# Half of the moving DFT tiles split by two GpSimd DMAs and a negated ScalarE copy instead of a ScalarE copy and a VectorE subtraction

## The chip, the cores and the metric

The kernel runs on one core of a Trainium2 chip, as one program. The metric is the device time of one execution in microseconds; the runs of the kernel before took 594.92, 598.23 and 600.19 us (median 598.23). A profile of one further execution gives the trace that is read below. The engines of the core are TensorE (PE, matrix products), VectorE (DVE), ScalarE (ACT), GpSimd (POOL) and SyncE (SP), each with its own queue of instructions that it works off in order. DMAs are issued from such a queue, and 16 DMA engines move the data.

## The reference

Two independent halves, whose outputs stand side by side in the last axis.

```python
# A: Fourier mixing, x is [1, 2048, 512]
a = einsum("bsd,ed->bse", x, dft_hid_re)
b = einsum("bsd,ed->bse", x, dft_hid_im)
y = einsum("ts,bse->bte", dft_seq_re, a) - einsum("ts,bse->bte", dft_seq_im, b)

# B: a diagonal state space model as a long convolution, u is [1, 2048, 512], N = 128
dt = exp(log_dt)
A = -exp(log_A_real) + 1j * A_imag
C = (C_real + 1j * C_imag) * dt[:, None]
P = exp((A * dt[:, None])[:, :, None] * pos[None, None, :])
K = 2.0 * einsum("dn,dnl->dl", C, P).real
y = irfft(rfft(u_t, 4096) * rfft(K, 4096), 4096)[:, :, :2048]
y = transpose(y) + u * D_skip
```

All inputs and outputs are float32.

## The kernel before

**The Fourier half (`Fnet`).** It multiplies in the other order than the reference: first `x` with the sequence matrices, then the result with the hidden ones. The sequence matrices come as 128 tiles `sT` of 128x512 (four stretches `t` of 512 output positions, two parts `c`, real and imaginary, 16 tiles `k` along the sequence). For each of the 8 groups `("s", t, c)`, the 16 tiles are the moving operands, the 16 resident `x` tiles the weights, and four PSUM tiles `acc` gather the result, which goes to DRAM as `p`. Four groups `("p", t)` of 8 tiles each follow: there the `p` tiles are moving and the hidden matrices `wT` are the weights. That is 8 x 16 + 4 x 8 = 160 moving tiles. The groups are worked off in the order s (all eight), then p.

Float32 products are made from three matmuls in a rounded 32-bit format, float32r. Every operand is split: `hi` is the operand rounded to float32r, `lo` is the operand minus `hi`, rounded as well. A product is `hi*x_hi + lo*x_hi + hi*x_lo` (L327). One moving tile takes part in 4 x 3 = 12 matmuls of 512 columns, so there are 160 x 12 = 1920 of them.

How a moving tile comes in (`load`, L287 on): SyncE's queue loads it into one of four `raw` buffers; when a slot of the ring of three `hi`/`lo` pairs is free, ScalarE copies `raw` into `hi` (L207) and VectorE writes `lo` as `raw - hi` (L211). The `raw` buffer is free after that, the ring slot after the last of the 12 matmuls.

**The other half (`Ssm`).** VectorE and ScalarE build two tables of powers per chunk of 32 channels (16 chunks; L566, L575, L582 and their neighbours), TensorE multiplies them into taps of the filter (L762), GpSimd adds the skip term to the first tap (L785, eight times), then come a two-stage transform of the taps (L792) and of `u` (L835), products of the spectra (L913 for the second stage, L926 to L942 for the products, L949 for the first inverse stage) and the last inverse stage (L995). Data passes through DRAM between the stages (`xu`, `xk`, `zs`). Its TensorE batches stand between the matmuls of the Fourier half.

**The order of the work.** A planner (`Plan`) runs the kernel as a set of coroutines: each step names an engine and an estimated duration, and the planner takes the step that can begin first, by urgency where several can. The instructions are written in that order, each engine's in the order of its steps. So the order is fixed when the kernel is built, from estimates: a DMA is taken to last 3.3 us (`LATENCY`) beyond its transfer, `load(kb)` is kb/330 us with a least value of 0.55, an ACT copy of 512 columns is 0.525 us. An engine that waits holds up what stands behind it in its own order. Semaphores of the planner stand for buffers: `raws` (4), `ss` (ring slots, `DEPTH`), `acc` (4 PSUM tiles), `ys` (3 staging tiles for evictions).


Of the kernel before, what the change touches and what calls it, by code (L numbers as in the profile page):

```python
# [8 lines left out]
F32 = mybir.dt.float32  # L9
F32R = mybir.dt.float32r  # L10
I32 = mybir.dt.int32
AF = mybir.ActivationFunctionType
OP = mybir.AluOpType
# [3 lines left out]
SEQ, DM, NS = 2048, 512, 128  # L17
# [151 lines left out]
def act(cols):  # L169
    return 0.09 + cols * 0.00085  # L170
# [6 lines left out]
def load(kb):  # L177
    return max(0.55, kb / 330)


class Fnet:
# [83 lines left out]
    def loads(self, b):  # L265
        yield b.uks
        x_raw = b.pool.tile([128, 4, DM], F32, name="uk", bufs=b.n)
        self.x_left = 16
        for g in self.groups:
            for i in self.items[g]:  # L270
                urgency = -1 if i in self.items[self.groups[0]][:3] else 0
                if g == self.groups[0]:
                    if i[3] >= 4:
                        yield self.x_ev[i[3] - 4]
                    if not i[3]:
                        self.plan.spawn(self.load_x0(x_raw[:, 0]), -1)
                    self.plan.spawn(self.load_x1(b, x_raw[:, i[3] % 4], i[3]), urgency)
                if i[0] == "p":
                    k = i[1], i[3] // 4, i[3] % 4
                    yield self.p_ev[k]  # L280
                    src = self.p[k]
                else:
                    src = self.sT[i[1], i[2], i[3]]
                yield self.raws
                self.plan.spawn(self.load(src, None, self.m, i, self.m_ev[i]), urgency)

    def load(self, src, to, where, key, ev):  # L287
        raw = self.pool.tile([128, DM], F32, name="raw", bufs=RAWS)
# [717 lines left out]


CHUNK, FIRST = 32, 128
RAWS, DEPTH, STAGED, AHEAD = 4, 3, 3, 3
BATCH = 2  # L1010


# [70 lines left out]
```

## Time and profile before

| | |
|---|---|
| median of the runs | 598.23 us (594.92 to 600.19) |
| span of the profiled execution | 595.6 us, 16944 instructions |
| TensorE busy | 585.1 us |
| VectorE busy | 495.7 us, 883 instructions |
| ScalarE busy | 381.0 us, 745 instructions |
| GpSimd busy | 5.3 us, 12 instructions |
| mean granted TensorE clock | 0.996 |
| DMA | 125.97 MB, 212 GB/s over the span |

The span is the time from the first to the last instruction of the profiled execution; the page gives no time around it, and the span lies within the times of the runs. "Busy" counts the time in which at least one instruction of an engine was under way; the ends of matmuls are modelled, and their recorded lengths overlap. A group row of the page gives line, engine, operation, destination and sources by name, shapes and count, then total busy time in us and the mean of one in ns, then the idle time of the engine just before these instructions and what ended most of it. A row of waits gives who waited for whom, the total in us, how often, and the longest.

### The profile page before, as it was taken

What the parts mean: (1) busy time and instruction counts of PE and PEld (TensorE: products, weight loads), DVE (VectorE), ACT (ScalarE), POOL (GpSimd) and SP (SyncE); (2) the same over time, 40 slices, a digit from 0 to 9 for tenths busy, and PEclk for the clock granted to TensorE, in tenths of its full rate; (3) what the DMA queues carried; (4) which work ended last, traced back from release to release, by engine and by line L of the source; (5) the groups of instructions that cost most, each with busy time, mean ns of one, the idle gap of its engine ahead of it and who ended that gap; (6) DMA issues with size and microseconds to landing.
All of it is one profiled execution on the core that took longest, in us unless ns stands there. A gap on an engine that the chain in (4) does not pass through costs nothing.

```text
span 595.6 us, 16944 instructions
## 1 busy us (share of the span) xinstructions
PE 585.1 (98%) x6982; PEld 451.6 (76%) x6982; DVE 495.7 (83%) x883; ACT 381.0 (64%) x745; POOL 5.3 (1%) x12
## 2 busy tenths in 40 slices
PE   8999999999999999999899999999989999999997
PEld 6767668788788777777687787778767887777775
DVE  6977989999999999999699999999979973253620
ACT  5789884947586596758374976677655625354522
POOL 0000000000000000000000000000000000000000
PEclk9999999999999999999999999999989999999999
DMA  8999995363593376454778593478668745899674
GB/s 264 321 360 344 333 339 186 107 177 94 128 279 100 102 193 216 141 148 122 237 213 245 149 279 120 132 213 257 207 202 253 249 126 168 223 348 276 204 256 149
DMA packets 141246, 125.97 MB, mean 212 GB/s; under 512 B 46192, under 2 KB 106352, under 8 KB 140912
## 3 DMA queue, kind: packets, MB, share of 16 engines
q1 hardware_dynamic: 140880, 124.48, 68.2%
q8 instruction: 55, 0.90, 0.6%
q10 hardware_dynamic: 288, 0.39, 0.3%
q14 instruction: 23, 0.19, 0.1%
HBM read 82.12 MB, written 42.73 MB: 210 GB/s over the span
## 4 chain that ended last, share of the span: by engine, by line
PE 79%; DVE 12%; DMA 3%; issue 3%; ACT 2%; SPq 0%; DVEq 0%; ACTq 0%
PE acc L327 61%; PE f L913 4%; PE f L762 4%; DVE prod L566 4%; PE f L995 3%; DVE lo L211 3%; PE f L835 3%; DVE t L575 3%; PE f L949 2%; PE f L792 2%; DMA raw<-in_sT 1%; DMA xt_u<-xu 1%; DVE z L929 1%; DMA p<-y 1%; DMA xt_k<-xk 1%
## 5 line engine op out<-in xcount | busy, mean ns | idle before, releaser
L327 PE MATMUL acc<-hi,x_hi 128*128 128x512 f32 x640 | 257.7, 403 | 3.7 <-ACT y L350 1.9
L327 PE MATMUL acc<-lo,x_hi 128*128 128x512 f32 x640 | 250.7, 392 | 0.1
L327 PE MATMUL acc<-hi,x_lo 128*128 128x512 f32 x640 | 250.0, 391 | 0.1
L566 DVE TENSOR_TENSOR prod<-t,cs 128x1024 f32<-128x1024 f32 (+4 forms) x192 | 164.1, 871 | 7.5 <-ACT t L704 5.6
L327 PEld LDWEIGHTS acc<-hi,x_hi 128*128 128x128 f32 x640 | 120.2, 188 | 49.6 <-issue 20.1
L211 DVE TENSOR_TENSOR lo<-raw,hi 128x512 fp32r<-128x512 f32 x160 | 109.4, 687 | 53.8 <-ACT hi L207 48.9
L207 ACT ACTIVATE hi<-raw 128x512 fp32r<-128x512 f32 x160 | 100.3, 628 | 76.9 <-PE acc L327 56.8
L327 PEld LDWEIGHTS acc<-hi,x_lo 128*128 128x128 f32 x640 | 120.5, 188 | 26.7 <-issue 0.6
L327 PEld LDWEIGHTS acc<-lo,x_hi 128*128 128x128 f32 x640 | 120.5, 188 | 24.3 <-DVE lo L211 1.4
L575 DVE TENSOR_TENSOR t<-prod 128x512 f32<-128x512 f32 (+4 forms) x192 | 94.3, 513 | 1.2
L582 ACT ACTIVATE square<-t 128x256 f32<-128x256 f32 (+1 forms) x64 | 36.5, 571 | 25.3 <-DVE t L575 23.2
L350 ACT ACTIVATE y<-acc 128x512 f32<-128x512 f32 x47 | 27.7, 595 | 17.3 <-PE acc L327 9.8
L926 ACT ACTIVATE uk<-f 128x1024 f32<-128x1024 f32 x32 | 31.6, 1015 | 6.4 <-PE f L913 6.4
L762 PEld LDWEIGHTS f<-t,t 128*32 128x32 f32 x2048 | 29.4, 110 | 6.5 <-issue 5.0
L762 PE MATMUL f<-t,t 128*32 128x64 f32 x2048 | 32.2, 220 | 0.3 <-issue 0.3
L929 DVE TENSOR_TENSOR z<-uk 128x512 f32<-128x512 f32 x32 | 22.0, 687 | 12.4 <-ACT uk L926 10.1
L641 ACT ACTIVATE cs<-cs 128x352 f32<-128x352 f32 x32 | 15.9, 536 | 17.9 <-DVE cs L636 17.9
L964 ACT ACTIVATE z<-f 128x512 f32<-128x512 f32 x32 | 17.7, 594 | 11.4 <-PE f L762 7.4
L595 DVE TENSOR_TENSOR t<-square 128x128 f32<-128x128 f32 (+1 forms) x64 | 24.8, 387 | 0.0
L913 PE MATMUL f<-xt_k,w 64*32 64x128 f32 x1024 | 23.1, 271 | 0.5 <-issue 0.5
L589 DVE SCALAR_TENSOR_TENSOR t<-t 128x128 f32<-128x128 f32 (+2 forms) x48 | 22.4, 467 | 0.3
L931 DVE TENSOR_TENSOR uk<-uk 128x512 f32<-128x512 f32 x32 | 22.1, 689 | 0.7
(85 smaller groups left out, 444.8 us busy)
## 6 DMA issues: line engine op xcount, KB each, us to landing
raw<-in_sT SPq DMA_DIRECT2D x127, 256.0 KB, 3.7
p<-y SPq DMA_DIRECT2D x32, 256.0 KB, 4.1
xt_u<-xu SPq DMA_DIRECT2D x32, 256.0 KB, 4.4
xk<-xk_sb SPq DMA_DIRECT2D x32, 256.0 KB, 4.0
xt_k<-xk SPq DMA_DIRECT2D x32, 256.0 KB, 5.5
zs<-z SPq DMA_DIRECT2D x32, 256.0 KB, 3.4
zl<-zs SPq DMA_DIRECT2D x16, 512.0 KB, 6.1
raw<-p SPq DMA_DIRECT2D x32, 256.0 KB, 4.2
```

Source lines behind the costliest of these rows:

```text
L207: self.nc.scalar.activation(hi, src, AF.Copy)
L211: self.nc.vector.tensor_tensor(lo, src, hi.bitcast(F32), op=OP.subtract)
L327: nc.tensor.matmul(acc[d], l[:, cols], r, start=k == 0 and n == 0, stop=k == len(items) - 1 and n == 2)
L350: self.nc.scalar.activation(y, ps, AF.Copy, scale=-1.0 if g[2] == 1 else 1.0)
L566: self.nc.vector.tensor_tensor(p.rearrange("p k d c m -> p k (d c) m"), src.rearrange("p d c l -> p (d c) l")[:, None, :, rows].to_broadca ...
L575: self.nc.vector.tensor_tensor(dst[:, :, :, rows], p[:, 0], p[:, 1, :, ::-1], op=OP.add)
L582: self.nc.scalar.activation(sq, t[:, :, :, m // 2:m], AF.Square)
L595: self.nc.vector.tensor_tensor(t[:, :, 0, m:2 * m:2], box[0][:, :, 0], box[0][:, :, 1], op=OP.subtract)
L762: nc.tensor.matmul(ps[32 * j:32 * j + 32, i], t1[:, d, c], t2[:, d, c], start=c == 0, stop=c == 1, tile_position=(0, 32 * j))
L913: nc.tensor.matmul(got[r][1][32 * xx:32 * xx + 32, g, o:o + PART], self.w2[rows, 2 * q + r, xx, 32 * c:32 * c + 32], xt[rows, r, xx], star ...
L926: a.activation(uk[:, r].rearrange("p g n c d -> p g (n c d)"), p, AF.Copy)
L929: v.tensor_tensor(P[:, r], t[:, r], u[:, r], op=OP.mult)
```

## The change

Of the S tiles, those with odd `k` in all groups but the first are split in another way (`soft` chooses them: 7 groups x 8 = 56 tiles). Such a tile takes a ring slot at once and no `raw` buffer. GpSimd's queue issues a DMA from DRAM into `hi`, whose type float32r differs from that of the source, so that the DMA converts; ScalarE then writes `-hi` into `lo`; then GpSimd's queue issues a second DMA of the same source tile that adds it to `lo`. The other 104 moving tiles, and `x` and `wT`, are split as before. The ring has five pairs in place of three, and the kernel is built with a smaller scratch area for the descriptors of GpSimd's DMAs (2048 bytes). To the planner, an issue on GpSimd's queue lasts 1.0 us.

```diff
@@ class Fnet, loads
                 else:
                     src = self.sT[i[1], i[2], i[3]]
+                if self.soft(i):
+                    yield self.ss
+                    self.plan.spawn(self.load_soft(src, i), urgency)
+                    continue
                 yield self.raws
                 self.plan.spawn(self.load(src, None, self.m, i, self.m_ev[i]), urgency)
+
+    def soft(self, i):
+        return i[0] == "s" and i[:3] != ("s", 0, 0) and i[3] % 2 == 1 and i[:3] <= SOFT_TO
+
+    def load_soft(self, src, i):
+
+        hi, lo = (self.pool.tile([128, DM], F32R, name=m, bufs=DEPTH) for m in ("hi", "lo"))
+        yield "pool", ISSUE
+        self.nc.gpsimd.dma_start(hi, src)
+        yield "dma", load(256)
+        yield "act", act(512)
+        self.nc.scalar.activation(lo, hi.bitcast(F32), AF.Copy, scale=-1.0)
+        yield "pool", ISSUE
+        self.nc.gpsimd.dma_start(lo, src, accum_op=OP.add)
+        yield "dma", load(256)
+        self.m[i] = hi, lo
+        self.split_ahead += 1
+        self.plan.set(self.m_ev[i])
@@ constants
-RAWS, DEPTH, STAGED, AHEAD = 4, 3, 3, 3
+RAWS, DEPTH, STAGED, AHEAD = 4, 5, 3, 3
+ISSUE, SOFT_TO = 1.0, ("s", 3, 1)
@@ def kernel
-    nc = bacc.Bacc("TRN2", target_bir_lowering=False, num_devices=1)
+    nc = bacc.Bacc("TRN2", target_bir_lowering=False, num_devices=1, dynamic_dma_scratch_size=2048)
```

## The prediction

> **What bounds the kernel now.** I read the busy shares first, then the 15 us windows of the whole core, then the chain that ended last, then the waits. The page's busy line and its DMA line:
>
> ```profile
> span 595.6 us, 16944 instructions
> PE 585.1 (98%) x6982; PEld 451.6 (76%) x6982; DVE 495.7 (83%) x883; ACT 381.0 (64%) x745; POOL 5.3 (1%) x12
> q1 hardware_dynamic: 140880, 124.48, 68.2%
> ```
>
> TensorE is idle for 595.6 - 585.1 = 10.5 us. The windows say where. Their columns are TensorE, weight loads, VectorE, ScalarE, GpSimd, granted clock, DMA share, GB/s:
>
> ```profile
> 0.00:15.00 15.00, 13.41 (x46) 9.86 (x47) 10.25 (x26) 7.78 (x13) 0.20 (x4) 1.00 0.85 265
> 45.00:60.00 15.00, 15.00 (x66) 11.28 (x65) 11.13 (x26) 14.85 (x35) 0.00 (x0) 1.00 1.00 345
> 60.00:75.00 15.00, 15.00 (x65) 9.24 (x64) 14.81 (x22) 12.82 (x26) 0.00 (x0) 1.00 0.97 329
> 75.00:90.00 15.00, 14.87 (x184) 10.48 (x181) 13.45 (x28) 13.15 (x28) 0.00 (x0) 1.00 0.91 343
> 90.00:105.00 15.00, 15.00 (x186) 12.42 (x185) 14.93 (x24) 7.21 (x17) 0.46 (x1) 1.00 0.54 168
> 270.00:285.00 15.00, 13.42 (x67) 9.82 (x59) 14.96 (x26) 11.62 (x21) 0.00 (x0) 1.00 0.58 161
> 285.00:300.00 15.00, 14.49 (x327) 11.43 (x328) 9.83 (x20) 6.23 (x16) 0.00 (x0) 1.00 0.74 214
> 405.00:420.00 15.00, 15.00 (x181) 12.35 (x165) 14.90 (x33) 11.10 (x23) 0.00 (x0) 1.00 0.94 285
> 435.00:450.00 15.00, 13.21 (x196) 10.14 (x199) 11.80 (x27) 7.55 (x16) 0.00 (x0) 0.89 0.69 203
> 585.00:600.00 15.00, 6.81 (x53) 5.21 (x51) 0.42 (x1) 3.42 (x7) 0.00 (x0) 0.89 0.45 141
> ```
>
> The head loses 15 - 13.41 = 1.6 us before the first operands are there, the tail 10.6 - 6.81 = 3.8 us for the last outputs. What is left between is 10.5 - 1.6 - 3.8 = 5.1 us: 2.1 of it between 270 and 300, 1.8 between 435 and 450. VectorE is at 14.9 of 15 us in the middle of the kernel, but TensorE is at 15.00 beside it: both are full, and TensorE is what adds up to the span.
>
> A busy TensorE could still be one that runs slowly. The chain's pieces (start, length, what) rule that out:
>
> ```profile
> PE 79%; DVE 12%; DMA 3%; issue 3%; ACT 2%; SPq 0%; DVEq 0%; ACTq 0%
> 4.52 23.45 PE acc L327 x96
> 27.97 1.92 PE f L835 x8
> 103.41 2.26 PE acc L327 x9
> 105.67 1.93 PE f L792 x16
> 125.88 21.30 PE acc L327 x93
> 147.19 1.93 PE f L762 x128
> 289.56 1.05 PE f L949 x32
> 296.10 1.96 PE f L913 x128
> 307.17 1.90 PE f L995 x32
> 435.08 1.78 issue
> ```
>
> Runs of 9 and 93 product matmuls differ by 84 matmuls and 19.04 us, so one costs 0.227 us and coming back from the other half costs about 0.2 us. A batch of the other half costs 1.05 to 1.96 us. **So the most that can be won is about 5 us, 0.9% of the span,** since the change removes no TensorE instruction.
>
> **The change part by part.** The rows of the split, and the waits around it:
>
> ```profile
> L211 DVE TENSOR_TENSOR lo<-raw,hi 128x512 fp32r<-128x512 f32 x160 | 109.4, 687 | 53.8 <-ACT hi L207 48.9
> L207 ACT ACTIVATE hi<-raw 128x512 fp32r<-128x512 f32 x160 | 100.3, 628 | 76.9 <-PE acc L327 56.8
> PEld acc L327 <- DVE lo L211: 1.4, 4, 0.6
> ACT hi L207 <- DMA raw<-in_sT: 1.5, 1, 1.5
> ```
>
> *VectorE.* Seven of the eight S groups have 8 odd tiles each, so 56 of the 160 subtractions go: 56 x 0.687 = 38.5 us of VectorE. All of it lies beside TensorE. TensorE's weight loads waited 1.4 us in total for those subtractions. Worth at most the two stalls that VectorE's chain leads to; the one at 435 is "issue", no engine's fault. The one in 270 to 300 ends behind these pieces of the chain:
>
> ```profile
> 277.47 1.28 ACT L623
> 279.13 0.95 ACT y L350 x2
> 280.62 3.84 DMA p<-y
> 284.54 0.60 ACT y L350
> 285.19 4.37 PE acc L327 x18
> ```
>
> An eviction came late in ScalarE's queue, then waited for a store. The freed VectorE and two more ring slots (ScalarE waited 56.8 us for TensorE to free a slot) make such a pile-up less likely. I take **-2 us** (between 0 and -5.1). The build's order shows what else the freed time does: the last tap batch moves forward by about 44 us of TensorE's work. That shifts work and removes none.
>
> *ScalarE.* 56 conversions become 56 negated copies of the same shape: no change in busy time. What is new is that such a copy waits for a GpSimd DMA. Behind it in ScalarE's order stand, in 46 of 56 cases, steps of the table chain, evictions or other copies out of PSUM, in 10 a conversion of the other kind (L207): whoever wants these waits too. The planner places the copy 1.0 + 256/330 + 3.3 = 5.1 us after the issue. With the same latency in the plan the 127 loads from SyncE's queue made ScalarE wait 1.5 us in all. I take **+2 us** (between 0 and 56 x 1 us).
>
> *The new path against the ring.* Both DMAs are strange to this trace: nothing goes through GpSimd's queue. The nearest rows (median from issue to landing):
>
> ```profile
> raw<-in_sT SPq DMA_DIRECT2D x127, 256.0 KB, 3.7
> zl<-zs SPq DMA_DIRECT2D x16, 512.0 KB, 6.1
> raw<-in_sT ACTq DMA_DIRECT2D x1, 256.0 KB, 3.1
> ib<-in_ib SPq DMA_DIRECT2D x1, 1024.0 KB, 9.2
> ```
>
> The converting one moves what a raw load moves: 3.7, and I add the plan's 1.0 for the issue. The adding one also has to fetch the 256 KB that it adds to, so I put it by the 512 KB row: 6.1 + 1.0. With the copy, 0.63, and about 0.4 for hand-overs the path is 4.7 + 0.6 + 7.1 + 0.4 = **12.8 us**; ends 3.1 + 0.6 + 3.1 + 0.4 = 7.2 and 2 x (9.2 + 1.0) + 1.0 = 21.4.
>
> How long may it be? In the changed order I counted for each of the 56 tiles TensorE's work from the last matmul that reads the slot's former tile to the first that reads the new `lo`, at the costs above. The shortest is 11.8 us, then 13.8, 13.8, 13.9, 15.0, eight of 16.0; the middle is 19.1, the longest 23.4. What a path overruns, summed over the tiles: 1 us for a path of 12.8, 3 for 14, 12 for 16, 25 for 17, 42 for 18, 103 for 20. A cliff, with its edge near 15. At 12.8: **+1 us**.
>
> *DMA.* By the queue's row, 0.682 x 595.6 / 124.48 = 3.26 us of all 16 engines per MB, so 0.85 us per 256 KB. Each of the 56 tiles adds one such transfer and the fetch of the addend, 1.7 us. Where the share is 0.5 to 0.7 that fits. It does not from 45 to 90 us, at 0.91 to 1.00: six of these tiles start between about 40 and 85 us, 10 us of transfers into 1.8 us of room, and the rest is pushed on to the loads, x, u and S, of SyncE's queue, until the 0.54 of the next window takes it up. 405 to 420 has two such tiles. I count half of the push as reaching TensorE, **+6 us** (between 0 and 12).
>
> Moved past: SyncE's queue loses 56 issues. GpSimd's queue holds the 8 skip additions (L785) between the DMAs; each can stand behind an adding DMA that waits for its copy, and L792 on TensorE follows it. That is within the +2.
>
> Sum: -2 + 2 + 1 + 6 = **+7 us** on 595.6, 602.6. The runs of before spread from 594.92 to 600.19 about 598.23, 2.6 above the span; +7 on that is **605**.
>
> The Trainium skill has its own price, in "DMA: Bandwidth & Descriptors", section "Anatomy of one DMA — SWDGE (gpsimd) path": about 2.0 us plus bytes over 436 GB/s for one GpSimd DMA. By that, an estimate, each takes 2.6 us, the path is 6.2, and the ring never stalls TensorE. The trace's SyncE loads, 3.7 us under load, lie above that.
>
> **The rivals.**
>
> *It is hidden, or a little faster.* For it: slack of 19.1 at the middle against 12.8; transfers from another queue need not stand behind SyncE's. Against: the full DMA windows. Point from which it decides: the path stays under 12 us and the push from 45 to 90 falls on work that nobody awaits, as the u tables are not wanted before the products. Then -2 + 0 to 3: 596 to 600. Faster by over 1% needs -6, more than the 5.1 that TensorE idles in between; the 1.7 us by which the first 96 matmuls (23.45 us) run behind 0.227 each don't help, since the first group is not touched.
>
> *Over the cliff.* The adding DMA is slower than a plain one of twice the bytes, or each half of the path takes over 7.5 us. For it: 6.1 to 9.2 us are in the table for bigger transfers, and TensorE's order is fixed, so one late tile holds all behind it. At a path of 17: 598 + 25 + 7 = 630; at 18, 647; at 20, 708.
>
> *GpSimd's queue is held up by VectorE.* VectorE is full, and its longest common instruction is this:
>
> ```profile
> L566 DVE TENSOR_TENSOR prod<-t,cs 128x1024 f32<-128x1024 f32 x96 | 117.1, 1221 | 1.1
> ```
>
> If each issue waited out one of these, the path grows by 2.4 to 15.2, the ring costs 8 in place of 1, and the time is 612. The skill's page "SBUF — State Buffer", section "SBUF: two separate sides", speaks for this: GpSimd cannot write descriptors while VectorE runs in a two-port mode. No run here shows it so far.
>
> *The change does not do what it says:* GpSimd takes so long per DMA that its queue is the bound. 56 tiles over some 400 us leave 3.6 us of GpSimd for each of the 112; at 5 us, 112 x 1.4 = 157 us more.
>
> **How the numbers follow.** 1%, 6 us, is about what can be told from no change here. The forecast, 599 to 614 in its own range, has 0.35; hidden 0.27; faster 0.07; the cliff 0.20; held up by VectorE 0.08; GpSimd the bound 0.03. Faster by over 1%: 0.07. Within 1% (592 to 604): the hidden case and about a quarter of the forecast, 0.36. Slower: 0.57. The range from 592 to 645 leaves out most of the faster case and what lies beyond a path of 18.
>
> **What would show it.** Right: L211 at 104 instructions and VectorE near 457 us; TensorE's busy matmul count unchanged; waits of L327 for the GpSimd DMA of a few us in total; DMA share up by some 10 points; windows 45 to 90 below 15.00 on TensorE. Wrong downward: no wait for GpSimd's DMAs and TensorE idle under 10 us. Wrong upward: an adding DMA that lands later than 8 us, and TensorE losing 1 us or more per such tile all along from 40 to 430 us.

## The result and the profile after

The changed kernel took 600.79 us (median, 597.17 to 604.26); the kernel before, timed beside it, 597.46 (594.92 to 600.56). The ratio is 1.0058 with a 95% interval from 1.003 to 1.0087: 0.6% slower, about 3.5 us. The forecast was 605 against 598.23, 1.1% slower: right in its sign, with twice the measured step. By the forecast's own bound of 1% the measured change counts as "within", to which it gave a chance of 0.36 against 0.57 for "slower".

The page of the changed kernel, in the order in which the page of before was read: busy shares, DMA queues, chain, groups, DMA issues.

```profile
span 599.8 us, 16969 instructions
PE 584.2 (97%) x6982; PEld 451.2 (75%) x6982; DVE 464.1 (77%) x827; ACT 380.6 (63%) x745; POOL 84.7 (14%) x124
q1 hardware_dynamic: 132816, 109.80, 59.5%
q0 software_dynamic: 16128, 29.37, 24.0%
PE 65%; issue 10%; DVE 10%; DMA 9%; ACT 3%; POOL 1%; SPq 0%; POOLq 0%; DVEq 0%; ACTq 0%
L211 DVE TENSOR_TENSOR lo<-raw,hi 128x512 fp32r<-128x512 f32 x104 | 71.4, 688 | 75.0 <-ACT hi L207 73.3
L303 POOL DMA_DIRECT2D lo<-in_sT x56 | 48.7, 870 | 164.7 <-ACT lo L301 146.2
L298 POOL DMA_DIRECT2D hi<-in_sT x56 | 32.7, 584 | 212.2 <-PE acc L349 97.0
L301 ACT ACTIVATE lo<-hi 128x512 fp32r<-128x512 f32 x56 | 34.9, 623 | 15.0 <-DMA hi<-in_sT 14.8
raw<-in_sT SPq DMA_DIRECT2D x71, 256.0 KB, 5.6
hi<-in_sT POOLq DMA_DIRECT2D x56, 256.0 KB, 5.3
lo<-in_sT POOLq DMA_DIRECT2D x56, 256.0 KB, 5.4
p<-y SPq DMA_DIRECT2D x32, 256.0 KB, 4.9
```

VectorE lost its 56 subtractions (L211 at 104) and 31.6 us of busy time, yet the span is 4.2 us longer. TensorE's share of the chain fell from 79% to 65%, and DMA rose from 3% to 9%. TensorE is idle for 599.8 - 584.2 = 15.6 us, 5.1 more than before. A store of `p` lands 4.9 us after its issue in place of 4.1, a `raw` load 5.6 in place of 3.7.

The windows of the changed kernel (TensorE, weight loads, VectorE, ScalarE, GpSimd, granted clock, DMA share, GB/s) say where TensorE's time went:

```profile
45.00:60.00 15.00, 15.00 (x65) 10.12 (x64) 11.44 (x26) 14.48 (x34) 2.28 (x3) 1.00 1.00 337
60.00:75.00 15.00, 15.00 (x66) 11.24 (x66) 14.76 (x24) 13.18 (x30) 2.71 (x5) 1.00 1.04 326
75.00:90.00 15.00, 15.00 (x184) 10.07 (x183) 12.40 (x25) 13.46 (x28) 2.21 (x3) 1.00 1.04 340
...
165.00:180.00 15.00, 12.65 (x167) 9.96 (x167) 13.09 (x26) 9.78 (x22) 1.43 (x2) 0.89 1.00 250
225.00:240.00 15.00, 13.14 (x59) 10.54 (x58) 13.33 (x24) 11.89 (x22) 2.83 (x4) 1.00 0.89 255
270.00:285.00 15.00, 15.00 (x185) 12.15 (x185) 14.54 (x30) 8.83 (x21) 2.84 (x4) 1.00 1.06 287
435.00:450.00 15.00, 15.00 (x211) 12.16 (x213) 13.02 (x22) 4.91 (x9) 4.24 (x6) 1.00 0.97 257
480.00:495.00 15.00, 13.71 (x295) 10.88 (x296) 6.63 (x11) 7.92 (x11) 0.00 (x0) 1.00 1.11 358
```

From 45 to 90 us, where the forecast put its largest term, TensorE is at 15.00 beside DMA engines that are full. The two stalls of before, in 270 to 285 and in 435 to 450, are gone. New ones stand at 165, 235 and 480, each in a stretch with a DMA share of 0.89 to 1.11. The waits of the changed kernel (who for whom; total, times, longest) say what TensorE stood for there:

```profile
PE acc L349 <- DMA lo<-in_sT: 3.9, 2, 2.3
PE acc L349 <- ACT y L372: 1.9, 1, 1.9
ACT y L372 <- DMA p<-y: 2.4, 2, 2.1
ACT lo L301 <- DMA hi<-in_sT: 14.8, 13, 2.8
```

TensorE waited 3.9 us for adding DMAs (at 165 and 480) and 1.9 us for an eviction (at 235). The other 4.4 us of its idle time between head and tail lie in gaps of 1.0 us and less. The timeline of the changed kernel around that eviction (start, length, engine, line, idle time before; some lines between are left out):

```profile
229.99 2.35 SPq L377 DMA_DIRECT2D p<-y  x3
232.94 0.50 ACT L641 ACTIVATE seed<-seed 128x352 f32<-128x352 f32 x1 [0.94 <-DVE seed L639]
233.98 1.28 ACT L643 ACT_TABLE_LOAD   x1
235.28 0.50 ACT L643 ACTIVATE seed<-seed 128x352 f32<-128x352 f32 x1
235.97 0.60 ACT L372 ACTIVATE y<-acc 128x512 f32<-128x512 f32 x1 [0.20 <-DMA p<-y]
236.62 0.50 PE L349 MATMUL acc<-hi,x_hi 128*128 128x512 f32 x1 [1.86 <-ACT y L372]
```

Three stores leave from 229.99 on, the fourth eviction needs one of the three staging tiles back, and TensorE needs the PSUM tile that this eviction frees. The first store landed only at 235.87, but ScalarE waited just 0.20 us for it: until 235.78 it was held by what stands before the eviction in its order, a wait of 0.94 us for VectorE, two seed steps, a conversion and a load of an activation table. With a faster store the eviction could have come 0.2 us sooner. The rest is its place in ScalarE's order, and no split tile is in this chain.

One reading of before was wrong. The forecast passed over a granted clock of 0.89 in two of the windows that it quoted. Seen finely, the stall at 165 shows what this is. The matmuls of the changed kernel behind it in the timeline, and its windows of half a microsecond (TensorE's busy time, clock, DMA share, GB/s):

```profile
167.66 0.79 PE L349 MATMUL acc<-lo,x_hi 128*128 128x512 f32 x1 [2.35 <-DMA lo<-in_sT]
168.25 0.63 PE L349 MATMUL acc<-hi,x_lo 128*128 128x512 f32 x1
168.68 0.63 PE L349 MATMUL acc<-hi,x_hi 128*128 128x512 f32 x1
```

```profile
167.00:167.50 0.50, 0.00 (x0) 1.00 1.21 299
167.50:168.00 0.50, 0.34 (x1) 0.65 0.92 194
168.00:168.50 0.50, 0.50 (x2) 0.50 1.21 212
...
170.50:171.00 0.50, 0.50 (x3) 0.50 1.16 320
171.00:171.50 0.50, 0.50 (x18) 0.94 1.18 308
```

After an idle gap of 2.35 us the clock is granted at one half for some 3.4 us, and matmuls start 0.43 us apart in place of 0.227: TensorE counts as busy, and 1.71 us more are lost. The stall of 1.78 us at 435 in the kernel before was followed by the same:

```profile
436.00:437.00 1.00, 0.14 (x1) 1.00 1.05 313
437.00:438.00 1.00, 1.00 (x3) 0.59 0.98 233
438.00:439.00 1.00, 1.00 (x9) 0.50 0.77 277
```

The other 0.89 of before, in the window from 585, costs nothing: TensorE's last matmul ends at 591.8, and the clock falls only after 594.0.

The Trainium skill, "TensorE: Matmul & The Clock Gate", section "What's actually happening", has such a gate: half rate after one idle window of 3413 ns, and full rate again after one busy window. The length of the slow stretch agrees with the trace. The onset does not: here gaps of 1.78 and 2.35 us were enough.

So each span can be taken apart into TensorE's idle time (span minus busy), the clock loss (one minus the granted clock, summed over half-microsecond windows up to TensorE's last matmul), and the rest. The rest is TensorE's work at full clock and, with it, waits too short to show as idle: a product matmul is recorded 0.39 us long, and the next starts 0.227 us after it. Profiled executions, us (the kernels from `ring5` on are those of the experiments below; `jitbefore2` and `jitafter2` are before and after in another order):

| kernel | span | idle | clock loss | rest |
|---|---|---|---|---|
| before | 595.6 | 10.5 | 1.7 | 583.4 |
| after | 599.8 | 15.6 | 1.7 | 582.5 |
| ring5 | 592.7 | 9.5 | 0.0 | 583.2 |
| nosub | 587.5 | 6.9 | 0.0 | 580.6 |
| noadd | 592.2 | 10.1 | 0.0 | 582.1 |
| ring6 | 604.9 | 19.5 | 0.0 | 585.4 |
| jitbefore2 | 602.1 | 16.5 | 5.1 | 580.5 |
| jitafter2 | 612.7 | 25.0 | 5.1 | 582.6 |

Between the two kernels the 4.2 us of span are +5.1 idle, 0.0 clock and -0.9 rest. In the middle, where head and tail are left out, before lost 5.1 idle and 1.7 clock, after 10.2 idle and 1.7 clock. The rest differs by up to 4.9 us between kernels with the same number of matmuls. No row says what ends these short waits, so differences in it stay unexplained.

### The profile page after: what moved, and what is told of

The parts are those of the page before. It is cut to its first block, busy times and chain, and to the rows that moved or that the text cites. A ratio compares the mean times of both kernels' runs of the same rounds, so it can differ in the third digit from the quotient of the medians.

```text
span 599.8 us, 16969 instructions
## 1 busy us (share of the span) xinstructions
PE 584.2 (97%) x6982; PEld 451.2 (75%) x6982; DVE 464.1 (77%) x827; ACT 380.6 (63%) x745; POOL 84.7 (14%) x124
## 4 chain that ended last, share of the span: by engine, by line
PE 65%; issue 10%; DVE 10%; DMA 9%; ACT 3%; POOL 1%; SPq 0%; POOLq 0%; DVEq 0%; ACTq 0%
PE acc L349 51%; DVE prod L588 4%; PE f L784 4%; PE f L935 3%; DMA hi<-in_sT 3%; PE f L857 3%; DVE t L597 2%; DMA lo<-in_sT 2%; PE f L971 2%; PE f L1017 2%; PE f L814 1%; DMA zl<-zs 1%; DMA par<-par_dram 1%; DMA p<-y 1%; DVE lo L211 1%
## 5 line engine op out<-in xcount | busy, mean ns | idle before, releaser
L588 DVE TENSOR_TENSOR prod<-t,cs 128x1024 f32<-128x1024 f32 (+3 forms) x192 | 164.2, 870 | 10.6 <-ACT t L726 6.0
L211 DVE TENSOR_TENSOR lo<-raw,hi 128x512 fp32r<-128x512 f32 x104 | 71.4, 688 | 75.0 <-ACT hi L207 73.3
L207 ACT ACTIVATE hi<-raw 128x512 fp32r<-128x512 f32 x104 | 65.2, 629 | 49.0 <-PE acc L349 39.5
L303 POOL DMA_DIRECT2D lo<-in_sT x56 | 48.7, 870 | 164.7 <-ACT lo L301 146.2
L298 POOL DMA_DIRECT2D hi<-in_sT x56 | 32.7, 584 | 212.2 <-PE acc L349 97.0
L301 ACT ACTIVATE lo<-hi 128x512 fp32r<-128x512 f32 x56 | 34.9, 623 | 15.0 <-DMA hi<-in_sT 14.8
L372 ACT ACTIVATE y<-acc 128x512 f32<-128x512 f32 x47 | 28.0, 596 | 25.8 <-PE acc L349 23.2
L935 PE MATMUL f<-xt_k,w 64*32 64x128 f32 x1024 | 23.2, 271 | 1.1 <-issue 0.9
```

What stands on the lines that cost most here:

```text
L207: self.nc.scalar.activation(hi, src, AF.Copy)
L211: self.nc.vector.tensor_tensor(lo, src, hi.bitcast(F32), op=OP.subtract)
L298: self.nc.gpsimd.dma_start(hi, src)
L301: self.nc.scalar.activation(lo, hi.bitcast(F32), AF.Copy, scale=-1.0)
L303: self.nc.gpsimd.dma_start(lo, src, accum_op=OP.add)
L588: self.nc.vector.tensor_tensor(p.rearrange("p k d c m -> p k (d c) m"), src.rearrange("p d c l -> p (d c) l")[:, None, :, rows].to_broadca ...
```

## The experiments

Three accounts were set against each other at first. Theory A, the forecast's: the added transfers crowd the DMA engines from 45 to 90 us and the rest is small. Rival B, the cliff: the path converting DMA, copy, adding DMA overruns the ring. Rival C: VectorE holds up GpSimd. All ratios are to the kernel before, timed beside the experiment.

### The ring alone, and VectorE's relief alone

`ring5` is the kernel before with the changed ring and scratch area, and no other edit.

```diff
-RAWS, DEPTH, STAGED, AHEAD = 4, 3, 3, 3
+RAWS, DEPTH, STAGED, AHEAD = 4, 5, 3, 3
-    nc = bacc.Bacc("TRN2", target_bir_lowering=False, num_devices=1)
+    nc = bacc.Bacc("TRN2", target_bir_lowering=False, num_devices=1, dynamic_dma_scratch_size=2048)
```

> The kernel before with a ring of five pairs and the smaller scratch area, no tile split by DMAs. If the loss of 3.3 us comes from the new DMAs (their engine time or their latency), this one is not slower than before: 594 to 598 us, TensorE idle 7 to 10.5 us. If it comes from the order that the planner makes with five slots, it is slower as the change is: 600 us or more, with stalls on TensorE for evictions and other tiles and none for a GpSimd DMA.

`nosub` goes one step on: the 56 tiles come in by SyncE's queue and through `raw` as before, but their subtraction is left out, and `hi` stands in for `lo` in the products. It shows what VectorE's relief is worth with no DMA added. (Its expectation speaks of a ring of three; the kernel that ran has five, as `ring5`.)

```diff
+            if self.soft(key):
+                hi, _ = (self.pool.tile([128, DM], F32R, name=m, bufs=DEPTH) for m in ("hi", "lo"))
+                yield "act", act(512)
+                self.nc.scalar.activation(hi, raw, AF.Copy)
+                self.plan.put(self.raws)
+                where[key] = hi, hi
...
+RAWS, DEPTH, STAGED, AHEAD = 4, 5, 3, 3
```

> Leaves out the subtraction for the same 56 tiles (their hi is used in place of lo) and adds no DMA: the relief of VectorE alone, ring of three. It gives the most that the relief can bring. My step put it at 2 us of at most 5.1: 593 to 596 us. If the relief of VectorE is worth nothing, 597.5; if the order that it leads to carries the loss, 600 us or more.

`ring5` took 594.86 us, ratio 0.9977 (0.9954 to 1.0); `nosub` 590.16, ratio 0.9907 (0.9893 to 0.9922). The page of `nosub`:

```profile
span 587.5 us, 16832 instructions
PE 580.6 (99%) x6982; PEld 450.3 (77%) x6982; DVE 461.8 (79%) x827; ACT 380.8 (65%) x745; POOL 6.2 (1%) x12
```

VectorE's relief and the ring are worth 0.93%, 5.6 us on 597, not the 2 us of the forecast. By the table the 8.1 us between the two profiled spans are 3.6 idle, 1.7 clock and 2.8 rest: more than "at most 5 us", because the bound counted only idle time. Between head and tail one gap of 0.9 us is left, and smaller ones. (In `nosub` the products of these tiles also wait for no `lo`. In the kernel before, TensorE's weight loads waited 1.4 us in all for the subtractions, so this adds little.)

### The second DMA without its addend

`noadd` is the changed kernel with a second DMA that overwrites `lo`. The addition is left out, and with it the fetch of what is added to; all else in the order stays.

```diff
-        self.nc.gpsimd.dma_start(lo, src, accum_op=OP.add)
+        self.nc.gpsimd.dma_start(lo, src)
```

> The change with the second GpSimd DMA overwriting lo (leaving out the addition): the same queue, the same conversion, the same waits, without the fetch of the addend. If the fetch is what makes the 112 DMAs take 24.0% of the engines, the share falls to about 18%, the landing of the second DMA by about 0.5 us, and the time by 1 to 3 us to 598 to 600. If the queue and the conversion make them dear, share and time stay: 24%, 600.8 us.

It took 596.83 us, ratio 1.0014 (0.9991 to 1.0036). Three lines of its page and one of its waits:

```profile
q0 software_dynamic: 16128, 29.37, 18.3%
hi<-in_sT POOLq DMA_DIRECT2D x56, 256.0 KB, 4.7
lo<-in_sT POOLq DMA_DIRECT2D x56, 256.0 KB, 4.3
PE acc L349 <- DMA lo<-in_sT: 0.3, 1, 0.3
```

The queue moves the same bytes, and takes 18.3% of 592.2 us for 112 DMAs: 0.97 us of the 16 engines for one that converts. Of the 24.0% of 599.8 us in the changed kernel, 56 x 0.97 are the first DMAs, so an adding one takes (143.9 - 54.3) / 56 = 1.60 us. SyncE's queue pays 0.85. The change then adds 0.97 + 1.60 - 0.85 = 1.72 us per tile, as forecast (1.7). With 0.63 us less per tile, TensorE's waits for `lo` fall from 3.9 to 0.3 us, and no stall is followed by the half clock. The one before the eviction near 235 is still there, at 1.08 us, behind the same steps of ScalarE. The time lies below the 598 to 600 us that were expected: the fetch cost more than its engine time suggested.

### Fewer tiles

`late` leaves the second group's eight tiles as before, so that the split by DMA starts after the windows from 45 to 90 have passed; `half` takes every fourth `k` in all seven groups, 28 tiles.

```diff
-        return i[0] == "s" and i[:3] != ("s", 0, 0) and i[3] % 2 == 1 and i[:3] <= SOFT_TO
+        return i[0] == "s" and i[:3] > ("s", 0, 1) and i[3] % 2 == 1 and i[:3] <= SOFT_TO
```

> The change with no split by DMAs in the second group either (48 tiles in place of 56), which takes the new DMAs out of the windows from 45 to about 85 us, where the DMA engines are full. My step put 5 us there: if it is right, 596 us. If the full windows cost nothing, since TensorE showed 15.00 in them, the time stays within what 8 of 56 tiles can bring: 600 to 601 us.

```diff
-        return i[0] == "s" and i[:3] != ("s", 0, 0) and i[3] % 2 == 1 and i[:3] <= SOFT_TO
+        return i[0] == "s" and i[:3] != ("s", 0, 0) and i[3] % 4 == 1 and i[:3] <= SOFT_TO
```

> The change with every fourth tile in place of every second (28 tiles, 56 DMAs): half of VectorE's relief, half of the added DMA time (share of the new queue 12%). If gain and loss both go with the count, about half way between the ring of five alone (594.9) and the usual place of the change (601 to 605): 598 to 600. If only crowding past some fill of the engines costs, it is faster than the ring alone: 592 to 594.

`late` took 606.78 us, ratio 1.0186 (1.016 to 1.0211): slower than all 56. `half` took 596.69, ratio 0.9996 (0.9973 to 1.0018). Neither time lies in a range that was expected for it. Theory A's place falls by the windows of the change, which show TensorE at 15.00 from 45 to 90 us; sparing them recovered nothing in `late` either. But a subset also gives the planner another order, so these two times decide little, and what the order does alone had to be measured (below).

### A deeper ring

`ring6` is the changed kernel with six pairs.

```diff
-RAWS, DEPTH, STAGED, AHEAD = 4, 5, 3, 3
+RAWS, DEPTH, STAGED, AHEAD = 4, 6, 3, 3
```

> The change with six pairs in the ring, which gives each tile about 3 us more between the freeing of its slot and its use. If late lo tiles at tight places of the ring are the cost (TensorE idle 3.9 us for them in the trace of the change), these waits go, and the time falls by 3 to 5 us to 596 to 598. If the DMA engines' time is, 600 to 601.

It took 605.54 us, ratio 1.0143 (1.0119 to 1.0168). In its waits TensorE no longer stands for any split tile's `lo`, and ScalarE stands longer for the first DMA and for stores of `p` (14.8 and 2.4 us in the change):

```profile
ACT lo L301 <- DMA hi<-in_sT: 24.3, 14, 3.5
ACT y L372 <- DMA p<-y: 7.4, 4, 4.8
```

Rival B asked for a gain once the ring gives more room. The waits for `lo` went and the time rose, so they are not what sets the end. TensorE's 19.5 us of idle time lie, beside head and tail, in eleven gaps of 0.6 to 1.8 us. Its time lies in neither expected range. It is also another order, so its 0.9% over the change can't be given to the deeper ring itself.

### The transfers without their consumers

`crowd` is `nosub` with both GpSimd DMAs added, into the `lo` tile that no product reads, so three transfers per tile.

```diff
+                self.nc.gpsimd.dma_start(lo, src)
+                self.nc.gpsimd.dma_start(lo, src, accum_op=OP.add)
```

> nosub (which has the ring of five, as the change) with a converting and an adding DMA per tile from GpSimd's queue added, into the lo slot that nobody reads; the raw loads stay, so three transfers per tile where the change has two. The order of TensorE, VectorE, ScalarE and SyncE is that of nosub, 590.2 us. It leaves out the subtraction. If the cost of the new path, 10.6 us between nosub and the change, is the DMA engines' time alone, the time rises by 8 us or more, to 598 or later, with SyncE's loads landing at 5 us and later. If it is the path as such, its length against the ring and the waits that stand in ScalarE's queue, the time stays within 3 us of nosub: 590 to 593.

It took 627.46 us, ratio 1.0503 (1.0456 to 1.055), 37 us above `nosub`. A row of its page and one of its waits:

```profile
L927 PE MATMUL f<-xt_k,w 64*32 64x128 f32 x1024 | 24.0, 290 | 12.0 <-DMA xt_k<-xk 10.7
```

```profile
DVE lo L211 <- DMA lo<-in_sT: 11.9, 4, 4.9
```

TensorE's largest wait, 10.7 us, is for loads of another stream, which land 6.9 us after their issue at the median, against 5.5 in the kernel before. So added transfers make transfers of others late enough to stall TensorE. Their price in the change is not shown, since the added DMAs also held ring slots (VectorE's 11.9 us) and each tile takes 0.85 + 0.97 + 1.60 = 3.42 us of the engines against 2.57.

### VectorE against GpSimd

`gpsub` is `ring5` with the 56 subtractions on GpSimd: a third place for the work, and a test of rival C with a GpSimd that computes.

```diff
+        if pool:
+            yield "pool", SUB, urgency
+            self.nc.gpsimd.tensor_tensor(lo, src, hi.bitcast(F32), op=OP.subtract)
+            return
```

> The ring of five and the subtraction of the same 56 tiles done by GpSimd in place of VectorE, with no DMA added: the relief of VectorE without the new path. The planner takes 1.3 us for one subtraction on GpSimd. If GpSimd needs about that and doesn't hold up VectorE, it comes near nosub: 590 to 593 us, faster than both kernels. If the two engines get in each other's way, VectorE's instructions grow longer (above 0.69 us for a 128x512 product) and it is not faster than 595.

It took 645.4 us, ratio 1.0825 (1.08 to 1.0851). Its groups, with shapes kept apart:

```profile
L215 POOL TENSOR_TENSOR lo<-raw,hi 128x512 fp32r<-128x512 f32 x56 | 131.5, 2352 | 370.0 <-ACT hi L210 289.9 <-DVE t L582 35.0 <-DVE prod L573 19.2
L573 DVE TENSOR_TENSOR prod<-t,cs 128x1024 f32<-128x1024 f32 x96 | 123.7, 1289 | 0.8
```

One subtraction takes 2.35 us there against 0.69 on VectorE, and VectorE's own 128x1024 products lengthen from 1221 to 1289 ns. So the two do hold each other up when GpSimd computes. When it only issues DMAs they do not: in the changed kernel the same products take 1220 ns, and an issue takes 0.58 or 0.87 us. Rival C falls for this change.

### The same kernels in other orders

`late` and `ring6` were slower than the change for no reason that their edit gives. `HOP` is a constant of the planner, its estimate of the hand-over between engines. Set to 0.31 or 0.29 it computes and moves the same and changes only the order in which the planner writes the instructions. This was done to the kernel before, the change, `ring5`, `nosub` and `noadd`.

```diff
-HOP, RESULT, LATENCY = 0.3, 0.15, 3.3
+HOP, RESULT, LATENCY = 0.31, 0.15, 3.3
```

> The kernel before with the same trifle in the planner (hand-over 0.31 us in place of 0.30): another order of the same work. If the scatter by order is a property of this planner, it moves by as much as the change did between 600.8 and 605.4, anywhere from 592 to 602. If the order is robust as long as no new DMA stands in it, it stays within 595 to 598.

> The change with one estimate of the planner moved by a trifle (the hand-over between engines 0.31 us in place of 0.30), which moves instructions and changes no work. It measures what the order alone does: if the loss belongs to the new DMAs, 599 to 603 us; if it is luck of the order, as the run without the second group's DMAs (606.8 us) makes one suspect, it may land anywhere from 594 to 607.

```diff
-HOP, RESULT, LATENCY = 0.3, 0.15, 3.3
+HOP, RESULT, LATENCY = 0.29, 0.15, 3.3
```

> The kernel before with the hand-over at 0.29 us: a second draw of the order without the change. As the run before it: 592 to 602 if the order scatters without the new DMAs, 595 to 598 if it does not.

> The change with the hand-over at 0.29 us: a third order with the new DMAs. If the measured 600.8 of the change is the lucky end and about 605 the usual place, 603 to 608; if 605.4 was the unlucky end, 598 to 602.

> The ring of five alone, hand-over 0.31 us. If the ring's 1.4 us gain is real and not a matter of order, 595 to 597.5 (1 us or more below the 598.1 of the kernel before at 0.31); if order, anywhere from 593 to 603.

> The ring of five alone, hand-over 0.29 us, beside 603.5 of the kernel before at this setting: 600 to 602.5 if the ring's gain holds, 593 to 603 if the order decides.

> The ring of five and no subtraction for the 56 tiles, hand-over 0.31 us. If VectorE's relief is real whatever the order, 4 to 6 us under the ring alone at 0.31, and within 2 us of the 590.2 at 0.30, since an engine with slack makes the order matter less. If it was luck, 594 to 600.

> The ring of five and no subtraction for the 56 tiles, hand-over 0.29 us: 589 to 592.5 if the relief makes the order matter less, 594 to 600 if the order decides here too.

> The change without the fetch of the addend, hand-over 0.31 us. If the fetch costs its 4 us whatever the order, 601 to 602 (605.4 less 4); if it costs by crowding, more where the order is worse: 597 to 600.

> The change without the fetch of the addend, hand-over 0.29 us, beside 615.2 of the change at this setting: 610 to 612 if the fetch costs 4 us everywhere, 600 to 607 if it costs more where the order is worse.

Ratios to the kernel before as it stands (each known to about 0.3%, `jitafter2` to 0.5%):

| `HOP` | before | ring5 | nosub | noadd | after |
|---|---|---|---|---|---|
| 0.30 | 1 | 0.9977 | 0.9907 | 1.0014 | 1.0058 |
| 0.31 | 1.0028 | 1.0011 | 0.9906 | 1.0021 | 1.0146 |
| 0.29 | 1.0106 | 1.0045 | 0.9905 | 1.0158 | 1.0302 |
| mean | 1.0045 | 1.0011 | 0.9906 | 1.0064 | 1.0169 |

In us, on 597, from column to column:

| step | at 0.30 | mean of three |
|---|---|---|
| ring of five | -1.4 | -2.0 |
| subtractions gone | -4.2 | -6.3 |
| two GpSimd DMAs in place of a raw load, no addend | +6.4 | +9.5 |
| the addend's fetch | +2.6 | +6.2 |
| sum | +3.5 | +7.4 |

All four steps keep their sign at each of the three settings: the ring and the relief gain, the DMAs cost more than both. With VectorE relieved and no DMA added no effect of the order can be told (0.9905 to 0.9907); in the kernel before it moves the time by 1.1%, in the change by 2.4%. Three settings are too few for an interval of the mean. The scatter was wider than expected: `jitbefore2` (603.54 us) and `jitafter2` (615.2 us) lie above every range given for them. `noadd_31` (596.22 us) lies just below its lower range, and `nosub_31` came out 6.8 us under the ring alone where 4 to 6 were expected. How the 6.4 us of the third step divide between the time of the DMA engines and the length of the path is not shown.

Where the change at 0.29 loses its time is in its waits:

```profile
PE acc L349 <- issue: 5.4, 3, 3.2
PE acc L349 <- ACT y L372: 5.1, 2, 3.2
PE f L784 <- issue: 2.9, 1, 2.9
PE acc L349 <- DMA lo<-in_sT: 0.9, 1, 0.9
```

Evictions and "issue" lead, the split tiles come last. Its gap before the eviction at about 235 us has grown from 1.9 to 3.2 us, and three gaps (this one of 3.24 us, and two of "issue" with 3.16 and 2.91 us) are each followed by the half clock, 5.1 us in all.

The waits name nothing that "issue" waits for, but the trace has more. The page of this run lists a DMA queue of the kind "instruction"; here it stands above one of the two long gaps:

```profile
q8 instruction: 55, 0.90, 0.6%
417.78 0.39 PE L349 MATMUL acc<-lo,x_hi 128*128 128x512 f32 x1 [3.16 <-issue]
```

Each of its 55 packets moves 16 KB. The 20 traces of this case have 66 stalls of TensorE above 0.4 us that are put down to "issue". In 65 of them the next matmul starts 1.20 to 1.65 us after such a packet ended (here 416.34), and in all 65 the number of TensorE's instructions up to there is 193 above a multiple of 256. So by all signs TensorE stood for its own instructions, which come through the DMA engines; why they come late is open. These stalls take 2.3 us in the kernel before (the one at 435 is among them), 2.9 in the change, 0.9 in `nosub`, but 7.1 in `jitbefore2` and 10.3 in `jitafter2`: most of the idle time that these two orders add.

## Why the prediction was right or wrong

**The sum.** It was -2 + 2 + 1 + 6 = +7. At the order that was timed, `nosub` to the change is 0.9907 to 1.0058, 9.0 us, as much as the forecast's 2 + 1 + 6. `nosub` against before is -5.6 us (-6.4 to -4.7) where the forecast had -2. So the step that failed in size is *VectorE*, "Worth at most the two stalls that VectorE's chain leads to", mis-sized by 3.6 us. That accounts for the difference between +7 and the measured +3.5. (`nosub` keeps the raw loads that the change drops, so the 9.0 is the net of the new path against them.) That the cost came out at 9 is luck: none of its three terms came out as it was argued, as the next paragraphs show.

**Why the bound was wrong.** "The most that can be won is about 5 us" took TensorE's busy time as work that can't shrink. It held 1.7 us of clock loss, visible as 0.89 in the quoted window from 435, and short waits that show as busy (the rest of `nosub` is 2.8 us smaller). The pieces of the chain that were meant to rule out a slow TensorE came from other places in the span. The stall at 435, put down as "no engine's fault" and worth nothing to VectorE, was worth 1.78 + 1.71 us, and it went in both `nosub` and the change. By the section before, it was a wait for TensorE's own instructions: no engine's fault indeed, but other orders did without it.

**DMA, +6.** Right in the engines' price (1.72 us measured per tile, 1.7 forecast; queue shares up from 68.2% to 83.5%), wrong in place. From 45 to 90 us the term is zero: the DMA engines are full and nobody awaits what they delay. That much the hidden rival had right. What the rows put down to DMAs came later, at 165 and 480, where the share is high and a `lo` tile is awaited. Half of a push in us of engine time was no measure for this; what counts is which transfer is late at a point without slack.

**The new path against the ring, +1.** TensorE waited 3.9 us for `lo`, and 1.7 more went to the clock behind the first of the two waits: 5.6. The length of the path was met, but not by its parts. From the first issue to the second landing it took 13.0 us at the median of the 42 tiles of which the trace has both landings (10.2 to 17.6), against a forecast of 12.8. The times to landing count from the start of the issue, so the forecast counted the issue twice; and the copy stood 1.3 us at the median in ScalarE's order behind the landing, for which the path had only the 0.4 of all hand-overs. One length for all tiles was the weak point: of the two that came late, one had a path of 14.9 us, the other, with 13.0, too little room. The estimate of 2.6 us per GpSimd DMA by the Trainium skill ("DMA: Bandwidth & Descriptors", section "Anatomy of one DMA — SWDGE (gpsimd) path") is not what these traces show: 5.3 and 5.4 us at the median in the change and 4.3 at the least, in `noadd`, beside a busy SyncE queue.

**ScalarE, +2.** Its copies waited 14.8 us for the first DMA, but the only wait of TensorE's products for ScalarE in the rows above is the eviction's 1.9, and in the timeline no split copy stands before that one. By these rows the term is near zero in this order.

**What would show it.** L211 at 104, TensorE's matmul count, a few us of waits for `lo`: right. VectorE was forecast near 457 and came to 464.1, though L211 lost the 38.0 us it should and the other rows hardly moved. Busy time counts overlapped instructions once: the lengths of all VectorE instructions sum to 38.6 us less (555.5 to 516.9), so the difference is less overlap. The DMA share rose by 15 points, not 10: the adding DMAs cost nearly twice a plain one, which the per-tile 1.7 had and the 10 points did not. The windows from 45 to 90 stayed at 15.00: wrong.

**The rivals.** The cliff fell: two waits in 56 tiles, and with a ring of six they are gone without gain. GpSimd held up by VectorE fell for DMA issues (0.58 and 0.87 us), and GpSimd as the bound with it (14% busy). The hidden case was right for the windows and wrong for the sum.

**What the forecast had no term for** is the order itself. A planner's constant moved by 0.01 shifts the kernel before by up to 1.1% and the change by up to 2.4%. The pair that was timed gives 0.6%, the pairs at the other settings 1.2% and 1.9%; the mean of the three kernels on each side differs by 7.4 us, close to the forecast's sum, though with gain (8.3 us) and cost (15.7 us) both larger than forecast.

No run points to a version of the change that beats both kernels beyond doubt. The ring of five without it comes nearest, at 0.9977 (0.9954 to 1.0) as timed and 0.3% under before in the mean of three orders. Choosing the tiles by the DMA share of their stretch was not tried.

## What to carry to other kernels

Moving work off an engine that is busy beside the bound can be worth more than the bound's idle time, since short stalls also lower TensorE's clock; read the granted clock of the windows before calling a busy TensorE full. Replacing a 0.69 us subtraction by a transfer was a poor trade here, where the DMA share is near 1 in stretches, and the late transfer need not be the one that was added (`crowd`). An eviction that follows a late store is not thereby late because of the store: look how long its engine waited for it, and what stood before it. In a kernel whose order is planned from estimates, time a change in several orders before an effect of 1% is put down to it.

## What the runs showed of the hardware

- By the queues' shares, a second DMA that adds into SBUF takes 1.60 us of all 16 engines per 256 KB, one that converts to float32r 0.97, a plain one on SyncE's queue 0.85. In `crowd` the converting and the adding one together take the same 2.6 us (23.2% of 624.1 us for 56 pairs).
- A TensorE gap can halve the granted clock for about 3.4 us (once 6.8, in `crowd`), at a price of 1.71 us. In these profiles such a fall followed gaps from 1.27 us (`half`, early in the span) to 4.6 us (`crowd`), and failed to follow others as long as 3.18 us (`gpsub`); no threshold in the gap's length alone separates them.
- GpSimd needs 2.35 us for a 128x512 float32 subtraction beside a busy VectorE, and VectorE's 128x1024 products take 6% longer meanwhile.
- TensorE's instructions come through the DMA engines in packets of 16 KB, and TensorE can stand still for them: 0.4 to 3.3 us at a time, shown as "issue", in 65 stalls of the 20 traces.
